# Three query groups of 128 and a 64-wide tail in one PV pass per pair, and a cubic exponential on VectorE for four tiles per batch entry

## The chip, the cores and the metric

The kernel runs on one core of a Trainium2 chip. The metric is the device time of one execution in microseconds. Each execution also records the mean clock that TensorE was granted, as a share of full speed.

A ratio below is the mean time of one kernel's fast runs over the mean of the fast runs of the kernel before from the same rounds on the same chip, so it isn't quite the ratio of the medians quoted beside it. Runs over 1.5% above the fastest run of the same kernel are called slow. On one core no second die tells whether such a run was disturbed from outside.

## The reference, cut to what matters

```python
def _attn_ref(q, k, v, cap):            # 8 batch entries, 12 heads, 448 rows, 64 wide
    scores = scale * np.matmul(q, k.transpose(0, 1, 3, 2))
    scores = cap * np.tanh(scores / cap)          # cap = 30
    attn = np.exp(scores - max);  attn /= attn.sum(-1)
    return np.matmul(attn, v)

def _moe_ref(x, phi, w1, w2):           # x: 3584 x 768, the attention output
    logits = x @ phi                              # 32 slots
    d = softmax of logits over the rows; slot_input = d.T @ x
    ...                                           # small two-layer MLP per expert, softmax over slots
```

Most of the time is attention: one tanh and one exponential for each of 8 x 12 x 448 x 448 elements, on ScalarE.

## The kernel before

Heads are worked in pairs, keys in tiles of 64. Two heads' 64 keys fill 128 partitions, so `ex` holds, for one key tile of a pair, 128 partitions by 448 queries. Six tiles make a step, 42 tiles (seven steps) make one batch entry, here called a period. The program order in the source is the order on each engine: there is no scheduler that moves instructions. VectorE's trace shows that order: the copy to kT started at 121.45 us, behind the polynomial operation that stands ahead of it, though its transposes had been issued from 120.09 to 120.61.

One step, on ScalarE two tanh and an exponential, on TensorE two passes of the PV product and two batches of score matmuls, with slots "a" to "d" for everything else:

```python
for j in range(NCH):
    tanh_chunk(2 * j); tanh_chunk(2 * j + 1); exp_chunk(j - 1)   # ScalarE
    pv_pass(pr, 0)                       # 14 matmuls, then rec and xq on VectorE
    run(j, "a")                          # x_transp; first part of the polynomial
    qk_chunk(2 * j + 2)                  # 6 score matmuls
    run(j, "b")
    pv_pass(pr, 1)                       # 14 matmuls, then rec and xq on VectorE
    run(j, "c")                          # second part of the polynomial
    qk_chunk(2 * j + 3)
    run(j, "d")                          # slot sums, zacc, transposes of K, fillers
```

The 448 queries are cut into four groups of 128 which overlap (offsets 0, 128, 256, 320); a mask keeps the doubled queries out of the softmax over rows. `spare(n)` issues n junk matmuls on TensorE ("fillers"). VectorE takes the exponential of one tile off ScalarE in some steps:

```python
shared = [j ... if j % 7 in (1, 3) and j > 7]

def poly_exp(j, part):                   # part 0: three operations (split into exponent and mantissa)
    ...
    elif part == 1:                      # two operations
        dve.scalar_tensor_tensor(xp, xm, POW2[1], xm, ALU.add, ALU.mult)
        dve.scalar_tensor_tensor(xp, xp, POW2[2], xm, ALU.add, ALU.mult)
    else:                                # two operations, a step later
        ...
for j in shared:
    for slot, part in (("a", 0), ("c", 1)):
        at(j, slot, poly_exp, j, part)
```

The small products (transposes of Q, K and x, logits, slot sums `slps`, row sums `zps`) all take their PSUM tile from a pool with a single buffer, psT; VectorE empties it each time. PV has a single bank too, psV.

The softmax here doesn't subtract the row's maximum and nothing guards it: scores larger than these inputs give would overflow.

## Time and profile before

| what | before |
|---|---|
| median time, 5 runs | 315.88 us (315.54 to 315.99) |
| mean granted clock | 0.981 |
| ScalarE / TensorE / VectorE busy | 89% / 87% / 61% |
| one period (42 key tiles) | 32.29 us, ScalarE without a gap |

The first two lines are the busy time of each engine on the page of the kernel before and the granted clock in 40 slices of the span, in tenths. It is at full until the very end.

```profile
PE 272.0 (87%) x4071; PEld 190.5 (61%) x4071; DVE 191.0 (61%) x478; ACT 278.9 (89%) x209; POOL 137.5 (44%) x178
PEclk9999999999999999999999999999999999999975
```

And a table by stage: one line for each step of a period, cut where the first score matmul of the step starts. After the colon-separated window come its length, the busy time of each engine with its number of instructions, the granted clock, the DMA share and GB/s. Shown are steps 5 and 6, and the sum over all seven steps.

```profile
core 0: us, PE busy (x) PEld busy (x) DVE busy (x) ACT busy (x) POOL busy (x), PEclk, DMA share, GB/s
126.61:131.72 5.11, 4.56 (x71) 3.31 (x71) 2.44 (x8) 5.11 (x4) 2.42 (x4) 1.00 1.06 204
131.72:136.14 4.42, 4.17 (x64) 3.01 (x62) 2.32 (x8) 4.42 (x4) 2.65 (x4) 1.00 1.17 175
...
sum 32.29, PE 29.39 PEld 21.03 DVE 21.78 ACT 32.29 POOL 16.96; mean PE 4.20 PEld 3.00 DVE 3.11 ACT 4.61 POOL 2.42
```

ScalarE is busy for the whole window, 32.29 of 32.29 us. TensorE is busy for 29.39 of them, at full clock.

### The profile page before, as it was taken

Reading aid. Unit: us, or ns where it says so; the run is one execution under the profiler, and the core shown is the slowest. Engines: PE = TensorE matmul, PEld = TensorE weight load, DVE = VectorE, ACT = ScalarE, POOL = GpSimd, SP = SyncE. Lnnn points to the kernel's source line nnn. Section 1 sums busy time; section 2 is a strip of 40 time slices with the busy share of each in tenths; the row PEclk is TensorE's granted clock in tenths of the full one; section 3 lists DMA queues with packets and bytes.
Section 4 is the critical chain, followed back from the end, with each engine's and each line's share of the span. In section 5 each row is a group of like instructions: output and inputs, shape, how many; then the busy total and the mean of one; then the engine's idle time right before and its main releaser. Section 6 shows DMA issues by size and latency. Waiting matters only on the chain.

```text
span 313.8 us, 9354 instructions
## 1 busy us (share of the span) xinstructions
PE 272.0 (87%) x4071; PEld 190.5 (61%) x4071; DVE 191.0 (61%) x478; ACT 278.9 (89%) x209; POOL 137.5 (44%) x178
## 2 busy tenths in 40 slices
PE   8899998989899989898989998989898898998710
PEld 6676666666676666666666666666676578643300
DVE  3624567846785578457855885578657765335830
ACT  4999999999999999999999999999999999226720
POOL 5593662655455654474457426652753020000000
PEclk9999999999999999999999999999999999999975
DMA  7999999799999999999999999999899829959996
GB/s 257 209 205 194 205 200 231 121 184 230 228 154 199 232 212 147 194 184 207 160 182 224 205 178 189 220 217 180 147 208 190 208 62 309 357 207 332 393 413 244
DMA packets 57481, 67.64 MB, mean 216 GB/s; under 512 B 3808, under 2 KB 53600, under 8 KB 57440
## 3 DMA queue, kind: packets, MB, share of 16 engines
q0 software_dynamic: 42448, 35.31, 73.5%
q1 hardware_dynamic: 14704, 31.50, 29.0%
q8 instruction: 32, 0.52, 0.6%
q10 hardware_dynamic: 288, 0.23, 0.2%
q14 instruction: 9, 0.07, 0.1%
HBM read 91.32 MB, written 18.87 MB: 351 GB/s over the span
## 4 chain that ended last, share of the span: by engine, by line
ACT 69%; PE 19%; DVE 5%; DMA 2%; issue 2%; DVEq 0%; ACTq 0%
ACT ex L291 36%; ACT ex L295 32%; PE pv L331 4%; DMA out_dram<-ob 2%; PE sc L282 2%; PE so_ps L690 2%; PE hp L662 2%; PE junk L521 2%; PE op L726 1%; PE boot L521 1%; DVE xq L342 1%; PE op L770 1%; ACT ob L779 1%; PE xps L357 1%; PE pvm L331 1%
## 5 line engine op out<-in xcount | busy, mean ns | idle before, releaser
L291 ACT ACTIVATE ex<-sc 128x1344 bf16<-128x1344 f32 (+1 forms) x113 | 163.7, 1719 | 0.8 <-PE sc L282 0.8
L295 ACT ACTIVATE ex<-ex 128x2688 bf16<-128x2688 bf16 (+4 forms) x58 | 158.0, 2753 | 0.1
L331 PEld LDWEIGHTS <-ex 128*128 128x128 bf16 x1344 | 78.0, 97 | 23.7 <-DVE xq L342 13.7
L331 PE MATMUL pv<-vbd,ex 128*128 128x130 bf16 x1274 | 89.2, 220 | 2.6 <-DVE xq L342 0.8
L282 PE MATMUL sc<-qT,kT 64*64 64x448 bf16 x672 | 78.6, 358 | 5.0 <-ACT ex L291 4.3
L260 POOL CAST vbd<-vraw 64x896 bf16<-64x896 f32 x23 | 22.4, 974 | 64.9 <-PE pv L331 49.8
L385 POOL COPY e<-E 128x512 bf16<-128x512 bf16 x9 | 6.7, 746 | 83.3 <-ACT E L379 49.2
L341 DVE RECIPROCAL rec<-pv 128x4 f32<-128x4 f32 x91 | 16.5, 182 | 42.6 <-PE pv L331 42.6
L342 DVE TENSOR_TENSOR xq<-pv,rec 128x256 bf16<-128x256 f32 x91 | 38.6, 424 | 3.1
L282 PEld LDWEIGHTS <-kT 64*64 64x64 bf16 x672 | 26.9, 105 | 22.2 <-issue 4.2
L521 PEld LDWEIGHTS <-ones 128*128 128x128 bf16 x428 | 26.0, 101 | 10.6 <-DVE xq L342 6.0
L521 PE MATMUL junk<-ones 128*128 128x128 bf16 x391 | 29.1, 220 | 3.1 <-DVE xq L342 2.6
L252 DVE COPY kT<-kps 128x896 bf16<-128x896 bf16 x23 | 14.3, 623 | 18.2 <-PE kps L250 18.0
L261 POOL CAST vbd<-vraw 64x896 bf16<-64x896 f32 x23 | 23.9, 1041 | 1.3
L109 POOL DMA_DIRECT2D w1b<-in_moe_w_dram x32 | 24.5, 766 | 0.0
L359 DVE COPY xT<-xps 128x512 bf16<-128x512 bf16 x47 | 19.5, 414 | 1.0 <-PE xps L357 1.0
L357 PE MATMUL xps<-ident,xq 128*128 128x128 bf16 x188 | 18.1, 218 | 0.8 <-DVE zacc L396 0.2
L172 POOL DMA_DIRECT2D qb<-in_q_dram x22 | 16.2, 737 | 3.9 <-DMA kraw<-in_k_dram 3.2
L252 DVE COPY qT<-qps 128x896 bf16<-128x896 bf16 x23 | 14.2, 618 | 5.5 <-PE qps L250 5.5
L250 PE MATMUL qps<-ident,qb 128*64 128x128 bf16 x308 | 12.8, 222 | 4.1 <-DVE lg L373 4.0
L172 POOL DMA_DIRECT2D kb<-in_k_dram x22 | 16.0, 727 | 0.0
L113 POOL DMA_DIRECT2D w2d<-in_moe_w_dram x20 | 15.1, 761 | 0.0
(117 smaller groups left out, 280.7 us busy)
## 6 DMA issues: line engine op xcount, KB each, us to landing
w1b<-in_moe_w_dram POOLq DMA_DIRECT2D x32, 384.0 KB, 8.5
vraw<-in_v_dram SPq DMA_DIRECT2D x23, 448.0 KB, 6.0
w2d<-in_moe_w_dram POOLq DMA_DIRECT2D x20, 384.0 KB, 9.4
w2t<-w2d SPq DMA_DIRECT2D x20, 384.0 KB, 5.2
out_dram<-ob SPq DMA_DIRECT2D x8, 768.0 KB, 8.5
qb<-in_q_dram POOLq DMA_DIRECT2D x22, 224.0 KB, 7.4
kb<-in_k_dram POOLq DMA_DIRECT2D x22, 224.0 KB, 7.8
w2b<-in_moe_w_dram POOLq DMA_DIRECT2D x12, 384.0 KB, 8.9
```

The costliest lines, as they stand in the source:

```text
L109: pool.dma_start(out=w1b[e][:, js, fs], in_=w1r[:, e, js, fs])
L172: (sp if nm == "v" else pool).dma_start(out=t, in_=quad_ap(nm, Q))
L252: dve.tensor_copy(t, ps)
L260: pool.tensor_copy(t[0:HP, :, :, 0:DH], raw[0:HP])
L261: pool.tensor_copy(t[HP:P, :, :, DH + 1:VW - 1], raw[HP:P])
L282: pe.matmul(sc[cs, u, 0:S], qkT["k", Q][r, c, cs], qkT["q", Q][r, :, cs], start=True, stop=True)
L291: act.activation(exs[j][:, half * CS + u0:half * CS + u1, :], sc[:, u0:u1, 0:S], ACT.Tanh, scale=qk_scale / cap)
L295: act.activation(exs[j][:, u0:u1, :], exs[j][:, u0:u1, :], ACT.Exp, scale=cap)
L331: pe.matmul(pvs[pr, half][:, n, 0:VW], exs[j][:, u, GOFF[g]:GOFF[g] + P], vbds[Q % 2][:, h, c, :], start=(c == 0 and n == 0), stop=(c == N ...
L342: dve.tensor_tensor(xq[Q][:, 2 * half:2 * half + 2, h * P:(h + 1) * P] .rearrange("p g (i d) -> p g i d", i=2), pv[:, :, :, 0:DH], rec.to_ ...
L357: pe.transpose(ps[:, g, :], xq[Q][:, g, h * P:(h + 1) * P], ident)
L521: pe.matmul(junk if home is None else home, ones, ones, start=True, stop=True)
```

## The change

Its intent: drop the overlap of the query groups (three groups of 128 plus a tail of 64 whose two heads sit on the two halves of the partitions), so that one PV pass per pair and one normalising pass are enough; make the polynomial one degree lower; and use the VectorE time won to take four tiles per period off ScalarE instead of two.

```diff
-GOFF = (0, 128, 256, 320)
+NF = 3;  TAIL = NF * P
-POW2 = (0.013534163, -0.157022653, 12.3105704, 23.0539684, 37.6797712)
+POW2 = (0.0780246108, -0.102619004, 6.12336670, 5.79476321)
-shared = [... if j % 7 in (1, 3) and j > 7]
+shared = [... if j % 7 in (1, 3, 4, 6) and j > 7]
         else:
-            dve.scalar_tensor_tensor(xp, xp, POW2[3], xm, ALU.add, ALU.mult)
-            dve.scalar_tensor_tensor(t, xp, POW2[4], xe.bitcast(F32), ALU.add, ALU.mult)
+            dve.scalar_tensor_tensor(t, xp, POW2[3], xe.bitcast(F32), ALU.add, ALU.mult)
...
+    def pv_rest(pr):
+        pv_mms(pr, CA, NT, (0, 1, 2), pvs[pr])            # 3 tiles x 3 groups of 128x130
+        for c0, c1 in ((0, CA), (CA, NT)):
+            pv_mms(pr, c0, c1, (NF,), pvs[pr][:, 2 * NF:NT, :])   # 14 tails of 64x65
+        norm(pr, 0, NT, pvs.pop(pr))                      # one pass over 448 columns
...
-            pv_pass(pr, 0)
+            pv_first(pr)                                  # 4 tiles x 3 groups
...
-            pv_pass(pr, 1, ...)
+            pv_rest(pr)
```

The transposes of x, the logits, the row sums and the slot sums follow the new grouping, and the mask goes (cut).

More of the change, by code (lines that the diff above doesn't have):

```diff
@@ L24 @@
 NG = 4
-GOFF = (0, 128, 256, 320)
-VW = 2 * (DH + 1)
-MASKED = -30000.0
-POW2 = (0.013534163, -0.157022653, 12.3105704, 23.0539684, 37.6797712)
+NF = 3
+TAIL = NF * P
+W = DH + 1
+VW = 2 * W
+POW2 = (0.0780246108, -0.102619004, 6.12336670, 5.79476321)
 @with_exitstack
@@ L78 @@
     pool.memset(ones32[0:NS, :], 1.0)
-    mask = consts.tile([P, NG, NS], F32, name="mask")
-    pool.memset(mask, 0.0)
-    pool.memset(mask[0:HP, NG - 1, :], MASKED)
     phib = consts.tile([P, NJ, NS], BF16, name="phib")
@@ L298, in exp_chunk @@
         exp_part(j, 1 if j in shared else 0, CH)
-    shared = [j for j in range(NCH - 2) if j % 7 in (1, 3) and j > 7] if cap < 80 else []
+    shared = [j for j in range(NCH - 2) if j % 7 in (1, 3, 4, 6) and j > 7] if cap < 80 else []
     def poly_exp(j, part):
@@ L315, in poly_exp, with pv_mms @@
         else:
-            dve.scalar_tensor_tensor(xp, xp, POW2[3], xm, ALU.add, ALU.mult)
-            dve.scalar_tensor_tensor(t, xp, POW2[4], xe.bitcast(F32), ALU.add, ALU.mult)
-    def pv_tiles(pr, half, c0, c1, home=None):
+            dve.scalar_tensor_tensor(t, xp, POW2[3], xe.bitcast(F32), ALU.add, ALU.mult)
+    def pv_mms(pr, c0, c1, gs, dst):
         Q, h = divmod(pr, 2)
-        if c0 == 0:
-            if h == 0 and half == 0:
-                xq[Q] = xs.tile([P, NG, 2 * P], BF16, name="xq", tag="xq")
-            pvs[pr, half] = psV.tile([P, 2, VW], F32, name="pv", tag="pv") \
-                if home is None else home
-        for c in range(c0, c1):
-            j, u = divmod(pr * NT + c, CH)
-            for n in range(2):
-                g = 2 * half + n
-                pe.matmul(pvs[pr, half][:, n, 0:VW],
-                          exs[j][:, u, GOFF[g]:GOFF[g] + P],
-                          vbds[Q % 2][:, h, c, :],
-                          start=(c == 0 and n == 0), stop=(c == NT - 1),
-                          skip_group_check=True)
@@ L337, in norm @@
-    def norm(pr, half):
-        Q, h = divmod(pr, 2)
-        pv = pvs.pop((pr, half))[:, :, 0:VW].rearrange("p g (i w) -> p g i w", i=2)
-        rec = xs.tile([P, 2, 2, 1], F32, name="rec", tag="rec", bufs=4)
-        dve.reciprocal(rec, pv[:, :, :, DH:DH + 1])
-        dve.tensor_tensor(
-            xq[Q][:, 2 * half:2 * half + 2, h * P:(h + 1) * P]
-            .rearrange("p g (i d) -> p g i d", i=2),
-            pv[:, :, :, 0:DH],
-            rec.to_broadcast([P, 2, 2, DH]), op=ALU.mult)
@@ L348, in pv_pass @@
-    def pv_pass(pr, half, home=None):
-        pv_tiles(pr, half, 0, NT, home)
-        norm(pr, half)
-    def x_transp(pr):
-        Q, h = divmod(pr, 2)
-        ps = psT.tile([P, NG, P], BF16, name="xps", tag="T")
-        for g in range(NG):
-            pe.transpose(ps[:, g, :], xq[Q][:, g, h * P:(h + 1) * P], ident)
-        t = xs.tile([P, NG, P], BF16, name="xT", tag="xT", bufs=2)
+        for tail in (False, True):
+            for c in range(c0, c1):
+                j, u = divmod(pr * NT + c, CH)
+                for g in gs:
+                    if (g == NF) != tail:
+                        continue
+                    for n in range(2 if tail else 1):
+                        r = slice(n * HP, n * HP + HP) if tail else slice(0, P)
+                        q0, s0 = g * P, 2 * (g - gs[0])
+                        out_, v_ = (dst[r, s0, :], vbds[Q % 2][r, h, c, n * W:n * W + W]) \
+                            if tail else (dst[:, s0:s0 + 2, :], vbds[Q % 2][:, h, c, :])
+                        pe.matmul(out_, exs[j][r, u, q0:q0 + (HP if tail else P)], v_,
+                                  start=(c == 0 and g == gs[0]), stop=(c == NT - 1),
+                                  skip_group_check=True)
@@ new lines, in norm, with xq_tile @@
+    def norm(pr, s0, s1, pv):
+        Q, h = divmod(pr, 2)
+        rec = xs.tile([P, NT, 1], F32, name="rec", tag="rec", bufs=4)[:, 0:s1 - s0, :]
+        dve.reciprocal(rec, pv[:, 0:s1 - s0, DH:W])
+        dve.tensor_tensor(xq[Q][:, h, s0:s1, :], pv[:, 0:s1 - s0, 0:DH],
+                          rec.to_broadcast([P, s1 - s0, DH]), op=ALU.mult)
+    def xq_tile(pr):
+        Q, h = divmod(pr, 2)
+        if h == 0:
+            xq[Q] = xs.tile([P, 2, NT, DH], BF16, name="xq", tag="xq")
+    CA = 4
@@ new lines, in pv_first, with turn_x @@
+    def pv_first(pr):
+        xq_tile(pr)
+        pvs[pr] = psV.tile([P, NT, W], F32, name="pv", tag="pv")
+        pv_mms(pr, 0, CA, (0, 1, 2), pvs[pr])
+    def pv_rest(pr):
[3 more added lines that the diff above has]
+        norm(pr, 0, NT, pvs.pop(pr))
+    def turn_x(ps, q0, pr, gs):
+        Q, h = divmod(pr, 2)
+        for g in gs:
+            c0 = g * P - q0
+            if g < NF:
+                pe.transpose(ps[:, c0:c0 + P],
+                             xq[Q][:, h, 2 * g:2 * g + 2, :].rearrange("p i d -> p (i d)"), ident)
+                continue
+            for n in range(2):
+                r = slice(n * HP, n * HP + HP)
+                pe.transpose(ps[r, c0:c0 + HP], xq[Q][r, h, NT - 1, :], ident[r, r])
@@ L359, in x_transp, with phi_mms @@
+    def x_transp(pr):
+        ps = psT.tile([P, S], BF16, name="xps", tag="T")
+        turn_x(ps, 0, pr, range(NG))
+        t = xs.tile([P, S], BF16, name="xT", tag="xT", bufs=2)
         dve.tensor_copy(t, ps)
         xTs[pr] = t
+    def phi_mms(dst, t, g, jt, first, last):
+        if g < NF:
+            pe.matmul(dst, t[:, g * P:(g + 1) * P], phib[:, jt, :], start=first, stop=last,
+                      skip_group_check=True)
+            return
+        for n in range(2):
+            pe.matmul(dst[n * HP:n * HP + HP], t[:, TAIL:S], phib[:, jt, :], start=first,
+                      stop=last, skip_group_check=True)
@@ L367, in logits @@
             for h in range(2):
-                pe.matmul(ps[:, g, :], xTs[2 * Q + h][:, g, :],
-                          phib[:, 2 * hq + h, :], start=(h == 0), stop=(h == 1))
+                phi_mms(ps[:, g, :], xTs[2 * Q + h], g, 2 * hq + h, h == 0, h == 1)
         xTs.pop(2 * Q), xTs.pop(2 * Q + 1)
@@ L372, in logits @@
             lgs[b] = xs.tile([P, NG, NS], F32, name="lg", tag="lg", bufs=2)
-        dve.tensor_tensor(lgs[b], ps, mask if hq == 0 else lgs[b], op=ALU.add)
+            dve.tensor_copy(lgs[b], ps)
+        else:
+            dve.tensor_tensor(lgs[b], ps, lgs[b], op=ALU.add)
     es, e4s = {}, {}
@@ L391, in e_norm @@
         for g in range(NG):
-            pe.matmul(ps, e4s[b][:, g, :], ones[:, 0:1], start=(g == 0), stop=(g == NG - 1))
+            r = slice(0, P if g < NF else HP)
+            pe.matmul(ps, e4s[b][r, g, :], ones[r, 0:1], start=(g == 0), stop=(g == NG - 1))
         if b == 0:
@@ L402, in e_transp @@
         ps = psT.tile([P, 512], BF16, name="eps", tag="T")
-        for g in (3, 0, 1, 2):
-            pe.transpose(ps[:, GOFF[g]:GOFF[g] + P], e4s[b][:, g, :], ident)
+        for g in range(NG):
+            n = P if g < NF else HP
+            pe.transpose(ps[:, g * P:g * P + n], e4s[b][0:n, g, :], ident[0:n, 0:n])
         dve.tensor_copy((ETl if b >= B - 2 else ET4[:, b // 2])[:, :, b % 2, :],
@@ L415, in e_sums, with slot_mms @@
         dve.reciprocal(winv[:, bb, :], ps)
-    def slot_mms(b, ps, gs, jts=None):
+    def slot_mms(b, ps, gs):
         for g in gs:
             for jt in range(NJ):
-                pe.matmul(ps[:, jt, :],
-                          xq[b * NQB + jt // 2][:, g, (jt % 2) * P:(jt % 2 + 1) * P],
-                          es[b][:, g, :], start=(g == 0 and jt == 0), stop=(g == NG - 1),
-                          skip_group_check=True)
+                x = xq[b * NQB + jt // 2][:, jt % 2, :, :]
+                if g < NF:
+                    pe.matmul(ps[:, jt, :], x[:, 2 * g:2 * g + 2, :].rearrange("p i d -> p (i d)"),
+                              es[b][:, g, :], start=(g == 0 and jt == 0), stop=False,
+                              skip_group_check=True)
+                    continue
+                for n in range(2):
+                    r = slice(n * HP, n * HP + HP)
+                    pe.matmul(ps[r, jt, :], x[r, NT - 1, :], es[b][r, g, :],
+                              start=False, stop=True, skip_group_check=True)
     def slot_sums(b):
@@ L446, in spare @@
     def spare(n):
-        busy(n, psV.tile([P, 2, VW], F32, name="junk", tag="pv")[:, 0, 0:P])
+        busy(n, psV.tile([P, P], F32, name="junk", tag="pv"))
     PER = 2 * NQB * NT // CH
@@ L549 @@
         if pr is not None:
-            pv_pass(pr, 0)
+            pv_first(pr)
         run(j, "a")
         if j == NCH - 1:
-            pv_pass(pr, 1)
+            pv_rest(pr)
             busy(8, psT.tile([P, P], F32, name="filler", tag="T"))
@@ L563 @@
         if pr is not None:
-            pv_pass(pr, 1, psT.tile([P, 2, VW], F32, name="pvt", tag="T")
-                    if pr == 0 else None)
+            pv_rest(pr)
         run(j, "c")
@@ L580, in bank @@
         return big.tile(shape, dt, name=name, tag="b")
-    pvm = [bank([P, 2, VW], name=f"pvm{half}") for half in range(2)]
-    pv2 = [bank([P, 2, VW], name=f"pvl{half}") for half in range(2)]
+    halves = [(0, 1), (2, NF)]
+    cuts = (0, 4, NT)
+    pvm = [bank([P, 4, W], name=f"pvm{half}") for half in range(2)]
+    pv2 = [bank([P, 4, W], name=f"pvl{half}") for half in range(2)]
     junk = bank([P, P], name="junk")
-    pv_tiles(last - 1, 0, 0, NT, pvm[0])
-    norm(last - 1, 0)
-    logits(NQ - 2)
-    pv_tiles(last - 1, 1, 0, NT, pvm[1])
-    norm(last - 1, 1)
-    for half in range(2):
-        pv_tiles(last, half, 0, NT - CH + CL, pv2[half])
-    x_transp(last - 1)
-    for half in range(2):
-        pv_tiles(last, half, NT - CH + CL, NT - 1)
-    for half in range(2):
-        pv_tiles(last, half, NT - 1, NT)
-        norm(last, half)
+    xq_tile(last - 1)
+    for half, gs in enumerate(halves):
+        pv_mms(last - 1, 0, NT, gs, pvm[half])
+        norm(last - 1, cuts[half], cuts[half + 1], pvm[half])
+        if half == 0:
+            logits(NQ - 2)
+    for half, gs in enumerate(halves):
+        pv_mms(last, 0, NT - CH + CL, gs, pv2[half])
+    x_transp(last - 1)
+    for half, gs in enumerate(halves):
+        pv_mms(last, NT - CH + CL, NT - 1, gs, pv2[half])
+    for half, gs in enumerate(halves):
+        pv_mms(last, NT - 1, NT, gs, pv2[half])
+        norm(last, cuts[half], cuts[half + 1], pv2[half])
     busy(5)
-    xl = xs.tile([P, NG, P], BF16, name="xT", tag="xT", bufs=2)
-    halves = [range(0, 2), range(2, 4)]
+    xl = xs.tile([P, S], BF16, name="xT", tag="xT", bufs=2)
     Q, bl = NQ - 1, B - 1
@@ L612 @@
         for g in gs:
-            pe.matmul(lps[s][:, g - 2 * s, :], xTs[2 * Q][:, g, :], phib[:, NJ - 2, :],
-                      start=False, stop=False, skip_group_check=True)
+            phi_mms(lps[s][:, g - 2 * s, :], xTs[2 * Q], g, NJ - 2, False, False)
     for s, gs in enumerate(halves):
-        hs = slice(2 * s, 2 * s + 2)
-        ps = bank([P, 2, P], BF16, name="xpl")
-        for g in gs:
-            pe.transpose(ps[:, g - 2 * s, :], xq[Q][:, g, P:2 * P], ident)
-        act.copy(xl[:, hs, :], ps)
+        q0, q1 = 2 * s * P, min(2 * s * P + 2 * P, S)
+        ps = bank([P, 2 * P], BF16, name="xpl")
+        turn_x(ps, q0, last, gs)
+        act.copy(xl[:, q0:q1], ps[:, 0:q1 - q0])
         busy(3)
     for s, gs in enumerate(halves):
-        hs = slice(2 * s, 2 * s + 2)
         for g in gs:
-            pe.matmul(lps[s][:, g - 2 * s, :], xl[:, g, :], phib[:, NJ - 1, :],
-                      start=False, stop=True, skip_group_check=True)
-        act.activation(el[:, hs, :], lps[s], ACT.Exp)
+            phi_mms(lps[s][:, g - 2 * s, :], xl, g, NJ - 1, False, True)
+        act.activation(el[:, 2 * s:2 * s + 2, :], lps[s], ACT.Exp)
     for gs in halves:
```

## The prediction

> **What bounds the kernel now.** I read the page first (busy shares, chain of waits), then the timeline of each engine over one period. A period is one batch entry b: 42 key tiles, worked off as seven steps of six tiles. I number the steps 0 to 6 by j mod 7. In each step ScalarE does two tanh of three tiles and one exponential of six (five where VectorE takes one over). TensorE does one PV pass, the score matmuls for the first half of a later step, another PV pass, and those for the second half.
>
> ```profile
> ACT 69%; PE 19%; DVE 5%; DMA 2%; issue 2%; DVEq 0%; ACTq 0%
> ```
> The chain is ScalarE's until about 222 us and then TensorE's. The period from 100.14 to 132.43 us on ScalarE, steps 3 to 5:
>
> ```profile
> 115.67 2.85 ACT L291 ACTIVATE ex<-sc 128x1344 bf16<-128x1344 f32 x2
> 118.02 2.85 ACT L295 ACTIVATE ex<-ex 128x2688 bf16<-128x2688 bf16 x1
> 120.35 0.71 ACT L379 ACTIVATE E<-lg 128x128 bf16<-128x128 f32 x1
> 120.55 2.87 ACT L291 ACTIVATE ex<-sc 128x1344 bf16<-128x1344 f32 x2
> 122.89 2.49 ACT L295 ACTIVATE ex<-ex 128x2240 bf16<-128x2240 bf16 x1
> 124.85 2.89 ACT L291 ACTIVATE ex<-sc 128x1344 bf16<-128x1344 f32 x2
> ```
> The starts, not the durations, give the rate, because the instructions overlap: two tanh 2.35, full exponential 2.33, short one 1.96 us. There is no gap, so ScalarE sets the 32.29 us period. But TensorE has little to spare: it waits for a score buffer (on ScalarE) only 0.3 to 1.0 us a period. Step 6 turning into step 0, on TensorE and then VectorE:
>
> ```profile
> 101.02 0.76 PE L282 MATMUL sc<-qT,kT 64*64 64x448 bf16 x6
> 101.70 0.25 PE L392 MATMUL zps<-ones,e 128*128 128x1 bf16 x4
> 102.21 0.58 PE L250 MATMUL kps<-ident,kb 128*64 128x128 bf16 x14 [0.25 <-DVE zacc L396]
> 102.72 0.98 PE L331 MATMUL pv<-vbd,ex 128*128 128x130 bf16 x14
> 103.53 0.39 PE L357 MATMUL xps<-ident,xq 128*128 128x128 bf16 x4
> 103.85 0.57 PE L282 MATMUL sc<-qT,kT 64*64 64x448 bf16 x6
> ```
> ```profile
> 101.12 0.18 DVE L341 RECIPROCAL rec<-pv 128x4 f32<-128x4 f32 x1 [0.84 <-PE pv L331]
> 101.34 0.42 DVE L342 TENSOR_TENSOR xq<-pv,rec 128x256 bf16<-128x256 f32 x1
> 101.99 0.16 DVE L396 TENSOR_TENSOR zacc<-zps,zacc 128x1 f32<-128x1 f32 x1 [0.23 <-PE zps L392]
> 102.83 0.62 DVE L252 COPY kT<-kps 128x896 bf16<-128x896 bf16 x1 [0.67 <-PE kps L250]
> ```
> TensorE and VectorE pass one PSUM bank (zps, kps, xps, lps, eps, slps, all in a pool of one buffer) back and forth: kps starts 0.06 us after zacc ends. VectorE runs in program order, so anything long put before such a copy stops TensorE. An example with the polynomial, step 1 (contended) and step 3 (not):
>
> ```profile
> 111.08 0.80 DVE L313 SCALAR_TENSOR_TENSOR xp<-xm 128x448 f32<-128x448 f32 x1
> 111.91 1.25 DVE L314 SCALAR_TENSOR_TENSOR xp<-xp,xm 128x448 f32<-128x448 f32 x1
> 120.26 0.62 DVE L313 SCALAR_TENSOR_TENSOR xp<-xm 128x448 f32<-128x448 f32 x1
> 120.91 0.62 DVE L314 SCALAR_TENSOR_TENSOR xp<-xp,xm 128x448 f32<-128x448 f32 x1
> 121.45 0.62 DVE L252 COPY kT<-kps 128x896 bf16<-128x896 bf16 x1
> ```
> ```profile
> 110.29 1.11 POOL L260 CAST vbd<-vraw 64x896 bf16<-64x896 f32 x1 [3.32 <-PE pv L331]
> 111.46 1.24 POOL L261 CAST vbd<-vraw 64x896 bf16<-64x896 f32 x1
> ```
> The pair of polynomial operations takes 2.01 us beside a GpSimd cast of V, 1.19 us alone.
>
> [...]the kT copy at 121.45 waited for L314 though kps had been issued from 120.09 to 120.61. [...]14 PV matmuls take 0.81 us to the next start before xps (same mode) and 0.91 before the scores (64*64). [...]24 slot matmuls at 124.53 take 0.61 us, 25 ns each.
>
> **The change, part by part.** (1) ScalarE. Shared tiles go from 14 to 27 (steps 1, 3, 4, 6 instead of 1, 3). Each shortens an exponential by 2.33 - 1.96 = 0.37 us: 13 x 0.37 = 4.8 us over the run; a period with four falls to 32.29 - 0.74 = 31.55 us.
>
> (2) PV on TensorE. A pair loses 7 full matmuls (58 ns each, 0.41 us) and gains 14 of 64x65. The K transposes in the small mode go at 0.51/14 = 36 ns; on separate row groups I take 30 ns: 14 x 30 = 0.42. Even. The tails stand next to the scores, which are 64*64 too[...]. The first part (12 matmuls) takes 0.70 us, the rest 9 x 58 + 100 + 420 = 1.04 us.
>
> (3) Small TensorE parts: 60 more matmuls a period in all, 42 of them the tails. Logits +0.2, slots +0.3 us (more matmuls, mode changes).
>
> (4) Normalising: two passes (0.56 us of VectorE each, start to next) become one over 448 columns. [...]one pass costs 0.76 us. Six pairs save 6 x 0.36 = 2.2 us a period, and the wait in the middle of a pair disappears.
>
> (5) Polynomial: first part, three operations, 1.16 us (109.37 to 110.53); second part 1.19 or about 2.0; last part now one operation, 0.62. Two more tiles add about 2 x 3.3 us and two dropped operations save 1.3. VectorE goes from 22.0 to about 25 us of a 31.5 us period: not full, but what matters is the order.
>
> In the built program the order of the changed kernel on VectorE in step 6 is xT, three polynomial operations, rec, xq, two polynomial operations, zacc, kT. In step 4: xT, last part, three operations, rec, xq, two operations, slacc. GpSimd's casts of V fall into steps 1, 4 and 6, right behind PV, so the second part is contended in both new steps.
>
> Now from the first score matmul of one step to that of the next (before, from the trace; after, worked by hand with the hand-over of 0.06 us to TensorE and 0.1 us back):
> - step 3 to 4: before 4.56, after 4.68 (longer multiply ahead of the kT copy).
> - 4 to 5: before 4.17. After: xT, last part and first part fill VectorE until 2.13; norm to 2.9; contended second part to about 4.4; slacc 4.75; xps, scores: 5.1.
> - 5 to 6: before 5.11. After: PV rest ends 1.63, q transposes 2.15, norm frees VectorE at 2.5, qT done 3.1, eps and ET to 4.0, logits, PV first, xps: 5.4.
> - 6 to 0: before 4.42. After: norm to 2.5, second part to 4.2 to 4.5, zacc, then kps 4.3 to 5.2, kT, xps: 5.9 to 6.3.
> - 0 to 1: before 4.75, after 4.9. 1 to 2: 4.48, after 4.4. 2 to 3: 4.80, after 4.4 (one operation fewer ahead of lg).
>
> Sum before: 32.29, ScalarE's pace. After: about 34.9 against ScalarE's 31.55. So the TensorE-VectorE loop would be the bound, 2.6 us a period slower than now. A score buffer may come late by 0.7 (after q transposes) to about 1.5 us before ScalarE stops, which shifts the first loss but not the rate. Six full periods (j from 8 on; the first has no polynomial) give 15.6 us, the last step 4 at the end about 1: 315.9 + 16.6 = 332.
>
> **The rivals.** (A) ScalarE stays the bound and the lag is absorbed: 315.9 - 4.8 = 311. For it: gapless ScalarE now, and VectorE only 80% busy. Against it: in step 6 alone kps moves from 1.2 to about 2.8 us after PV ends, where the slack is 0.7. (B) The loop lengthens, but tails cost less than 30 ns and casts miss the second part (1.2 us): my steps then sum to about 33.3, 315.9 + 6 x 1.0 = 322. (C) Tails cost 60 ns, as if nothing overlapped: 0.42 more a pair, 2.5 a period where TensorE is the pace: towards 340. The 36 ns of the small-mode transposes speak against it. (D) The chain after 267 us changes: only a few norms and small matmuls, under 1 us.
>
> **Range and chances.** The hand chain gives 332, its mild form 322, ScalarE's bound 311. I lean on the chain but not on all of it, since each step has 0.2 us of guess and the rival forms lie below: 326 us, 8 in 10 between 314 and 334. The 2% line is at 309.6 and 322.2. Faster needs more than the whole 4.8 us on ScalarE: 0.04. Within 2%: 0.30. Slower: 0.66.
>
> **What would show it.** Right: the chain of waits moves from ScalarE to TensorE and VectorE; ScalarE shows idle time at tanh, released by the score matmuls, mostly in steps 0, 1 and 6; kps waits on zacc for 1.5 us or more; periods of 33 to 35 us. The group of the second polynomial part shows a mean near 0.8 and 1.1 us. Wrong: ScalarE without gaps and a period near 31.6; PV tails far from 30 ns; or kps not behind the second part.

## The result, and the profile after

| | before | after |
|---|---|---|
| median of 5 runs | 315.88 us | 359.16 us (356.37 to 367.9) |
| ratio of fast runs | | 1.134 (1.130 to 1.138) |
| mean granted clock | 0.981 | 0.91 in the fast runs, 0.87 in the profiled one |

The changed kernel is correct and 13% slower; the prediction's range ended at 334. The profiled run was the slowest of the five (366.1 us from first to last instruction). What I read from it below is a pattern, not a size; sizes are taken from runs with a steady clock.

These are lines of the page of the changed kernel: ScalarE's busy tenths, the granted clock, the engines of the chain that ended last, and the group of the tanh.

```profile
ACT  4999999659967699549967699548988998623740
PEclk9999999559975799559976899558999999999995
PE 54%; DVE 28%; ACT 13%; issue 2%; DVEq 0%; ACTq 0%
L289 ACT ACTIVATE ex<-sc 128x1344 bf16<-128x1344 f32 (+1 forms) x113 | 141.5, 1298 | 50.7 <-PE pv L330 42.4
```

The second line was flat before. Now it dips to half several times, and each dip of ScalarE's line sits under or next to one. The chain moved from ScalarE (69% before) to TensorE and VectorE, as predicted. ScalarE stood still for 50.7 us ahead of its tanh (0.8 us before). The tanh writes into one of four `ex` buffers, and PV is what frees them: the page puts 42.4 us down to PV and only 7.2 to the score matmuls, which the prediction had named as the releaser. The same table by stage for steps 5 and 6, with the sum of the period:

```profile
146.35:154.48 8.13, 7.65 (x84) 5.11 (x83) 3.06 (x7) 4.99 (x4) 1.19 (x2) 0.52 1.13 203
154.48:162.98 8.50, 7.02 (x73) 4.85 (x73) 4.80 (x10) 4.91 (x4) 5.39 (x7) 0.50 0.25 62
...
sum 41.04, PE 35.51 PEld 24.18 DVE 25.48 ACT 32.22 POOL 17.73; mean PE 5.07 PEld 3.45 DVE 3.64 ACT 4.60 POOL 2.53
```

The two steps run at a clock of 0.52 and 0.50, and take 8.13 and 8.50 us instead of 5.11 and 4.42. TensorE is nearly always busy in step 5 (7.65 of 8.13 us): this isn't waiting, its work takes longer. What went ahead of the fall is on TensorE's timeline (the bracket is the idle time before the group and what ended it):

```profile
144.72 0.84 PE L330 MATMUL pv<-vbd,ex 128*128 128x130 bf16 x12 [1.11 <-POOL vbd L259]
146.09 0.33 PE L365 MATMUL xps<-ident,xq 128*128 128x128 bf16 x3 [0.52 <-DVE slacc L467]
...
160.35 0.96 PE L248 MATMUL kps<-ident,kb 128*64 128x128 bf16 x14 [1.48 <-DVE zacc L425]
```

In step 4 TensorE waits twice within 2.5 us. The profile puts the first wait down to GpSimd's cast of V, because that ended last (144.61); the norm, which frees the single PV bank, ended at 144.57. It is the norm that counts: in a variant below without a tile in step 4, the same PV group started at 130.63, 0.2 us after the norm (130.41) and well before the cast ended (131.49). What made the norm late, and slacc and zacc after it, is on VectorE's timeline:

```profile
142.79 1.00 DVE L309 TENSOR_SCALAR xe<-xe 128x448 int32<-128x448 int32 x1
...
145.14 0.62 DVE L312 SCALAR_TENSOR_TENSOR xp<-xp,xm 128x448 f32<-128x448 f32 x1
145.68 0.35 DVE L467 TENSOR_TENSOR slacc<-slps,slacc 128x192 f32<-128x192 f32 x1
...
158.97 1.25 DVE L312 SCALAR_TENSOR_TENSOR xp<-xp,xm 128x448 f32<-128x448 f32 x1
160.15 0.15 DVE L425 TENSOR_TENSOR zacc<-zps,zacc 128x1 f32<-128x1 f32 x1
```

VectorE does exactly what the prediction said it would: the second part of the polynomial stands ahead of slacc in step 4 and ahead of zacc in step 6, and TensorE's next product into psT starts when slacc or zacc frees the bank: xps at 146.09 us where slacc ended at 146.03, kps at 160.35 where zacc ended at 160.30. Cut into stretches of 3.5 us, the same place one period later reads:

```profile
184.00:187.50 3.50, 1.87 (x46) 1.54 (x44) 3.00 (x6) 3.50 (x3) 3.44 (x5) 1.00 1.20 182
187.50:191.00 3.50, 3.50 (x47) 2.31 (x44) 1.69 (x4) 1.31 (x2) 1.03 (x2) 0.52 1.13 229
```

TensorE was busy for only 1.87 of 3.50 us, and in the next stretch the clock is at half. The clock reads 1.00 or 0.50 wherever a stretch lies wholly in one state, and the six stretches at half during attention, with their edges interpolated within the quarter of a microsecond in which the clock changes, last 17.07 (three times), 10.24, 3.41 and 20.48 us in this run. These are 5, 5, 5, 3, 1 and 6 times one length of 3.413 us (an estimate from them: 20.48 / 6), which I call a clock window below.

So there were two theories for the missing time. Theory 1: the chain through VectorE is as predicted, and its waits also trip the clock, which the prediction never considered. Theory 2: the new grouping of PV (more and smaller matmuls, mode changes) is slow by itself, and the clock with it. Against both stands a third: that the clock comes from outside, from a bad chip or moment.

### The profile page after: what moved, and what is told of

It reads as the page before. It is cut to its first block, busy times and chain, and to the rows that moved or that the text cites.

```text
span 366.1 us, 10324 instructions
## 1 busy us (share of the span) xinstructions
PE 306.5 (84%) x4551; PEld 207.6 (57%) x4551; DVE 211.4 (58%) x450; ACT 279.7 (76%) x209; POOL 138.9 (38%) x176
## 4 chain that ended last, share of the span: by engine, by line
PE 54%; DVE 28%; ACT 13%; issue 2%; DVEq 0%; ACTq 0%
PE pv L330 16%; PE sc L280 10%; ACT ex L289 6%; DVE xq L338 5%; ACT ex L293 5%; PE junk L557 5%; DVE xp L312 4%; DVE xp L311 3%; PE xps L365 3%; DVE xe L309 3%; PE qps L248 3%; PE kps L248 2%; PE xps L370 2%; PE so_ps L723 2%; PE lps L382 2%
## 5 line engine op out<-in xcount | busy, mean ns | idle before, releaser
L289 ACT ACTIVATE ex<-sc 128x1344 bf16<-128x1344 f32 (+1 forms) x113 | 141.5, 1298 | 50.7 <-PE pv L330 42.4
L293 ACT ACTIVATE ex<-ex 128x2688 bf16<-128x2688 bf16 (+4 forms) x58 | 128.1, 2212 | 0.1
L330 PE MATMUL pv<-vbd,ex 128*128 128x130 bf16 (+1 forms) x1610 | 100.3, 228 | 9.2 <-POOL vbd L259 7.8
L330 PEld LDWEIGHTS <-ex 128*128 128x128 bf16 (+1 forms) x1680 | 84.3, 111 | 40.7 <-issue 33.4
L280 PE MATMUL sc<-qT,kT 64*64 64x448 bf16 x672 | 93.4, 398 | 1.3 <-ACT ex L289 1.1
L376 DVE COPY xT<-xps 128x448 bf16<-128x448 bf16 x47 | 18.3, 390 | 38.1 <-PE xps L370 38.1
L338 DVE TENSOR_TENSOR xq<-pv,rec 128x448 bf16<-128x448 f32 x46 | 28.7, 625 | 1.6
L312 DVE SCALAR_TENSOR_TENSOR xp<-xp,xm 128x448 f32<-128x448 f32 x27 | 25.1, 929 | 0.9
L248 PE MATMUL kps<-ident,kb 128*64 128x128 bf16 x308 | 14.7, 242 | 10.0 <-DVE zacc L425 8.6
L311 DVE SCALAR_TENSOR_TENSOR xp<-xm 128x448 f32<-128x448 f32 x27 | 17.5, 648 | 0.0
```

Of the source, the lines that this page charges most:

```text
L248: pe.transpose(ps[h * HP:h * HP + HP, c, :], src[:, h, c * DH:(c + 1) * DH], ident)
L280: pe.matmul(sc[cs, u, 0:S], qkT["k", Q][r, c, cs], qkT["q", Q][r, :, cs], start=True, stop=True)
L289: act.activation(exs[j][:, half * CS + u0:half * CS + u1, :], sc[:, u0:u1, 0:S], ACT.Tanh, scale=qk_scale / cap)
L293: act.activation(exs[j][:, u0:u1, :], exs[j][:, u0:u1, :], ACT.Exp, scale=cap)
L330: pe.matmul(out_, exs[j][r, u, q0:q0 + (HP if tail else P)], v_, start=(c == 0 and g == gs[0]), stop=(c == NT - 1), skip_group_check=True)
L338: dve.tensor_tensor(xq[Q][:, h, s0:s1, :], pv[:, 0:s1 - s0, 0:DH], rec.to_broadcast([P, s1 - s0, DH]), op=ALU.mult)
```

## The experiments

Sixteen kernels ran, all with correct results, three rounds each (four runs of each kernel with the profiled one). The kernel before ran beside them each time at 315.6 to 315.8 us, which already speaks against the third theory. Edits are against the changed kernel unless the text says otherwise.

### Which part of the change costs the time?

**Two tiles again, everything else kept.**

```diff
-    shared = [... if j % 7 in (1, 3, 4, 6) and j > 7]
+    shared = [... if j % 7 in (1, 3) and j > 7]
```

> The changed kernel with the regrouping and the cubic kept, but only the old two tiles per period on VectorE (steps 1 and 3). Theory 1 (the two extra tiles, placed in steps 4 and 6 ahead of the small copies that TensorE waits for, make the loop long and let TensorE idle so that its clock is granted at half): without them the clock stays at 1.00 through the attention and the time is that of before, 315 to 317 us. Theory 2 (the regrouping, with its 480 more matmuls and its mode changes, is what costs): the time stays well above 330 us.

Measured: 317.69 us, ratio 1.009 (1.005 to 1.013), clock 0.98, no dip. The grouping, the single norm and the cubic cost 1.8 us together (2.0 against the kernel before of the same rounds, 315.65 us), and don't touch the clock. Theory 2 falls. Part of the 1.8 us is in the tail of attention, where ScalarE waits longer for the last transposes of x; this is ScalarE's line of waits (total, times, longest) of the kernel before, then of this one:

```profile
ACT xT L620 <- PE xpl L619: 1.8, 1, 1.8
```
```profile
ACT xT L655 <- PE xpl L365: 3.4, 1, 3.4
```

**The kernel before with the cubic and four tiles.** Old groups, two PV passes:

```diff
-    (1, 3)            # in before
+    (1, 3, 4, 6)      # and the new POW2, with the merged last operation
```

> The kernel before, with its 4 x 128 groups and two passes, given the cubic and four tiles per period. Theory 1: the same wait of the K transposes on the zacc copy and the same half clock appear, 345 us or more, since the two-pass kernel has no less work on VectorE. Theory 2: the tiles are harmless, so the time is at or under 316 us.

Measured: 352.03 us, ratio 1.099 from the two fast runs (345.42 and 347.95 us; the other two took 356), clock 0.91 to 0.95 from run to run. So the four tiles with the cubic, without any of the new grouping, bring most of the loss: the wait of the K transposes on zacc reached 2.2 us, and in its profiled run the clock fell five times before the end of attention.

### Is it the clock, and what lowers it?

**The waits filled with junk matmuls.** VectorE's order is untouched; TensorE gets 49 fillers a period, in the places where it waits.

```diff
+        if 0 < b < B - 1:
+            at(j + 6, "d", spare, 22)         # before the K transposes
+            at(j + 11, "d", fill, 18)         # before the slot sums
             at(j + 11, "d", slot_sums, b)
+            at(j + 11, "d", spare, 9)         # after them
```

> The changed kernel with 49 meaningless matmuls added per period, in the places where TensorE sat idle in steps 4 and 6 (18 ahead of the slot sums, 9 ahead of the next PV, 22 ahead of the K transposes). Nothing waits for them. Theory 1: TensorE no longer idles there, the granted clock stays at 1.00, and what is left is the loop at full clock, the 34.9 us a period of the hand chain or a little more: 328 to 338 us, although there is more work. Theory 3 (the loop is as long as it is because of waits, and the half clock only fills time that would be waited anyway): no better than 355 us.

(The recorded text's theory 3 is not the third theory above, but that the half clock costs nothing of its own.) Measured: 341.77 us, ratio 1.085, clock 0.98 to 0.99. The granted clock of its page:

```profile
PEclk9999999999999999999999999999999999999975
```

More work on TensorE made the kernel 17.4 us faster (359.16 to 341.77), because it held the clock (0.98 to 0.99 against 0.91). It came out above the 328 to 338 us that I expected, since the loop itself is longer than my hand chain had it (by step, further below). The junk itself costs little: from step 4 to 5, which both kernels run at full clock, the loop takes 5.80 us with it and 5.69 without. This run splits the loss: about 1.8 us for the grouping (two tiles), about 24.1 us for the chain through VectorE at full clock (341.77 - 317.69), about 17.4 us for the clock; what the junk costs is counted with the chain.

**The kernel before with nothing but a delay.** The kernels so far differed in grouping and polynomial. These take the unchanged kernel before and put 2, 4 or 6 fills of a scratch tile on VectorE ahead of zacc in step 6 of six periods (measured at 432 ns each), the last also with junk matmuls in the wait:

```diff
+        for _ in range(2):                    # or 4, or 6; in e_norm, in before
+            dve.memset(xp, 0.0)
         if b == 0:
             dve.tensor_copy(zacc, ps)
```
```diff
+        if 0 < b < B - 1:                     # fourth run only, with 6 fills
+            at(j + 6, "d", spare, 26)
```

> The kernel before with two VectorE fills of a scratch tile (an estimated 0.43 us each) ahead of zacc in step 6 of six periods. The K transposes should wait about 0.9 us instead of 0.25. If a single wait must come to about 1.5 us in 3.5 us to lower the clock: clock stays at 0.98, 316 to 318 us. If any wait near 1 us lowers it: half-clock stretches and over 320.

> The same with four fills: a wait of about 1.75 us. If idleness summed over a stretch of some 3.5 us decides, and where the stretch begins is chance: the clock falls in some periods and not in others, different from run to run, mean clock 0.94 to 0.98, 320 to 332 us. If waits cannot lower the clock without the changed grouping or polynomial: clock 0.98, 319 to 323.

> The same with six fills: a wait of about 2.6 us. If idleness decides: the clock falls in most of the six periods, mean clock 0.90 to 0.95, 330 to 345 us. If not: clock 0.98, 323 to 328.

> Six fills as in the run before, and 26 junk matmuls on TensorE in five of the waits. If idleness lowers the clock: clock at 0.97 or above, 322 to 329 us, although VectorE is as late as before. If the delay itself (VectorE's load) lowers it: the same time and clock as without the junk matmuls.

| fills | longest wait on zacc | time | clock of the four runs |
|---|---|---|---|
| 0 (before) | 0.3 us | 315.62 us | 0.98 |
| 2 | 1.0 us | 317.07 us | 0.979 to 0.983 |
| 4 | 2.1 us | 332.53 us | 0.945 to 0.965 |
| 6 | 3.3 us | 342.46 us | 0.934 to 0.941 |
| 6, with junk matmuls | 1.8 us | 331.30 us | 0.972 to 0.982 |

Windows of 3.5 us around the wait, in the kernels with 2, 4 and 6 fills:

```profile
99.50:103.00 3.50, 2.55 (x34) 1.58 (x36) 2.24 (x7) 3.50 (x3) 1.80 (x2) 1.00 1.18 184
```
```profile
103.00:106.50 3.50, 1.36 (x23) 0.83 (x21) 2.35 (x7) 3.50 (x4) 3.03 (x4) 1.00 1.24 203
106.50:110.00 3.50, 3.50 (x38) 2.48 (x34) 1.56 (x4) 2.22 (x1) 1.79 (x3) 0.51 1.20 266
```
```profile
142.50:146.00 3.50, 0.64 (x10) 0.30 (x7) 2.63 (x7) 3.50 (x4) 3.46 (x5) 0.96 0.99 158
```

With TensorE busy for 2.55 of 3.50 us the clock stays; with 1.36 the next stretch runs at 0.51. With four fills the clock fell after the wait in all six periods of the profiled run, and came back after 3.5 us five times and after 7 us once. Six waits of one microsecond cost 1.5 us in all, six of two microseconds 16.9: six more microseconds of waiting cannot be that step. The last run closes it: with VectorE just as late but junk matmuls in the wait (in all six waits, not five), the clock is back and 11.2 us are won, though 331.30 us is above the 322 to 329 that I expected. The wait left there is 1.8 us, and its profiled run still shows one fall in six: that wait lies near the edge. That idleness of TensorE lowers the clock, in the kernel before as in the changed one, is thereby shown.

### Which of the waits trips it?

**Three variants with one of the two new steps disarmed.** First the tile of step 4 left out (tiles 1, 3, 6), then the tile of step 6 (tiles 1, 3, 4), then all four tiles with only step 4's second part moved behind slacc:

```diff
-    (1, 3, 4, 6)
+    (1, 3, 6)                                 # first;  (1, 3, 4) second
```
```diff
-        for slot, part in (("a", 0), ("c", 1)):
+        for slot, part in (("a", 0), ("d" if j % 7 == 4 else "c", 1)):     # third
```

> The changed kernel with tiles in steps 1, 3 and 6 only, in their old places. The wait of the K transposes on zacc in step 6 stays, about 1.5 us. At full clock the hand chain gives about 34.0 us a period, 325 to 330 us. If one wait of 1.5 us in a period is enough to halve the clock, some periods are longer and it lies between 330 and 345 us.

> The changed kernel with tiles in steps 1, 3 and 4 only, in their old places. What is left are the two waits of step 4 (1.1 us ahead of PV, 0.5 us ahead of the x transposes); in the full change the clock fell right after these. At full clock the hand chain gives about 33.9 us a period, 324 to 330 us. If these two waits are what makes the clock fall, it falls here too, once a period, but comes back within about 4 us since step 6 has no long wait: 328 to 340 us.

> The changed kernel with only step 4's second part moved behind slacc; step 6 stays as in the change. If the pair of waits in step 4 (1.1 us on the norm and 0.5 us on slacc) is what trips the clock, removing the second of them keeps it at full: about 326 to 331 us, with the wait of the K transposes on zacc of 1.5 us or more still there, clock 0.97 or above. If the wait of step 6 trips it by itself: half-clock stretches stay, 340 us or more.

| variant | waits left in a period | time (runs) | clock |
|---|---|---|---|
| no step 4 | 2.1 on zacc | 331.16 (329.01 to 335.37) | 0.965 to 0.980 |
| no step 6 | 1.1 and 0.5 in step 4 | 357.14 (335.13 to 361.27) | 0.863 to 0.971 |
| step 4's second part late | 1.1 in step 4, 2.1 on zacc | 346.03 (343.34 to 348.88) | 0.929 to 0.957 |

Three of the four runs of the second variant count as slow by the rule above, so it has no ratio; its clock differs from run to run, and even its fastest run stands at 335.13 us. I had expected one culprit, the pair of waits in step 4, for the third kernel 326 to 331 us, and for the second a fall of about 4 us a period and at most 340 us. Both expectations failed: both places can do it. In the profiled run of the first variant the clock fell in one period of six, though the wait was about the same in all. This stretch of it has TensorE busy for 1.60 us and was not followed by a fall:

```profile
105.50:109.00 3.50, 1.60 (x33) 1.36 (x35) 2.43 (x4) 3.43 (x3) 3.42 (x5) 1.00 1.23 205
```

But I cut this stretch by hand, and the clock windows lie elsewhere. The clock record shows where: in each trace with falls, all changes of the clock lie whole multiples of 3.413 us apart (in the changed kernel 5, 12, 17, 24, 29, 36, 39, 40, 41, 48 and 54 windows after the fall at 64.78 us). In this variant one boundary is at 106.15 us. The gap from 105.35 to 107.40 us was shared by two windows, with TensorE busy for 2.60 and 2.16 of 3.41 us, and the clock held. The gap from 70.01 to 72.07 us lay all but 0.06 us in one window, with 1.41 us busy, and the clock fell at 72.01. The other four gaps straddle a boundary too, and none had a fall. In this trace, then, the gap that lay in one window was followed by a fall, and the five that were shared by two were not.

The runs also differ in length of the fall: after step 4's waits the clock mostly stayed low for 10.2 to 20.5 us, after the one wait on zacc for 3.4 to 6.8. Busy time doesn't tell these apart: two windows of the changed kernel at half clock were both busy for 3.41 of 3.41 us, and the clock stayed low after the first (187.66 to 191.07 us) and came back after the second (194.49 to 197.90). At full clock, the windows just ahead of this run's falls were busy for 1.36 to 2.04 us, but the clock also held after one with 1.85 (279.82 to 283.23). What goes along with it is the work done. For each matmul that starts in a window, take the columns it streams times the share of the 128x128 array that it uses; add up, with the shapes and windows of all 18 profiled traces (1309 windows, from 18 us on to about the end of attention). All 56 windows under 2590 were followed by half the clock and all 1135 over 3240 by full, whichever clock they ran at themselves; the 118 between went both ways. The two windows above count 2742 and 2908. At half clock a window holds less work: in the changed kernel, from 20 to 290 us, a median of 2616 (998 to 3558) against 4189 at full. This is a pattern in the traces; no run varied the work of a window at the same busy time. That a kernel near this edge can stay low because of it is my reading, and was not shown.

### Is the rest VectorE's order?

**All four tiles, the second part behind slacc and zacc.**

```diff
-        for slot, part in (("a", 0), ("c", 1)):
+        for slot, part in (("a", 0), ("d" if j % 7 in (4, 6) else "c", 1)):
```

> The changed kernel with the second polynomial part of steps 4 and 6 moved from before to behind the small copies (slacc; zacc and kT) in VectorE's order. Same work, no extra matmul. Theory 1: the K transposes no longer wait on zacc for more than 0.5 us, the clock stays at 1.00 or nearly, and by the same hand chain a period takes about 33 us: 315 to 325 us. If VectorE's total load is the cause and not its order: unchanged, over 350 us.

Measured: 324.38 us, ratio 1.028 (1.026 to 1.030), clock 0.98 to 0.99: 34.8 us of the loss gone with the same instructions in another order. TensorE at the K transposes, then VectorE:

```profile
71.42 0.58 PE L248 MATMUL kps<-ident,kb 128*64 128x128 bf16 x14 [0.25 <-DVE zacc L423]
```
```profile
71.21 0.16 DVE L423 COPY zacc<-zps 128x1 f32<-128x1 f32 x1
72.04 0.62 DVE L250 COPY kT<-kps 128x896 bf16<-128x896 bf16 x1 [0.67 <-PE kps L248]
```

The wait on zacc is back at the 0.25 us of the kernel before. The 1.1 us wait in step 4 stayed, and the clock held: one such wait a period did not lower it here. Moving step 3's second part as well:

> The changed kernel with all four tiles, second part late in steps 3, 4 and 6, all fillers. If VectorE's order is what costs, a little better than the run with only steps 4 and 6 late: 319 to 324 us. If the remaining wait is VectorE's sheer amount of work in step 4 (the first part ahead of the norm), the same as that run: 323.5 to 325.

It gave 320.76 us (ratio 1.016; one of its four runs took 326.94), within the expected 319 to 324. Four tiles thus stay slower than before in every order I tried; the first part of step 4 still stands ahead of the norm.

### Is there a version that beats both?

**Fewer fillers.** With the second part late in all new steps, I took out 30 of the 36 fillers a period, to give TensorE room, once with four tiles and once with three:

```diff
-        at(j + 1, "d", spare, 10);  at(j + 2, "a", spare, 14);  at(j + 2, "c", spare, 8);  at(j + 3, "d", spare, 4)
+        at(j + 2, "a", spare, 6)
```

> Four tiles; the second polynomial part of steps 3, 4 and 6 behind the small copies; 30 of the 36 filler matmuls a period taken out. The fillers now stand in a loop that sets the pace, so taking them out should shorten steps 1 to 3 by 1.0 to 1.5 us and the late part of step 3 another 0.5: a period between ScalarE's 31.55 and 32.2 us, 311 to 317 us, if the clock stays at 1.00. If the fillers are needed to keep the clock, it falls in steps 1 to 3 and the time is over 330 us.

> As the kernel with four late tiles, but three (steps 1, 3, 6), so without the contended first part of step 4. ScalarE's period is 31.92 us and no step should exceed it by much: 313 to 315.5 us with a full clock; over 330 if the clock falls in steps 1 to 3.

Neither reached its time: 347.35 us (clock 0.84 to 0.90, two of four runs slow), where the other branch of the expectation, over 330 us, came true; and 319.26 us (0.92 to 0.94, one run slow), where neither branch did. The fillers look like waste, and they are what keeps the clock up in steps 2 and 3: in a period of the three-tile run it was at half from 115.28 to 125.5 us, between the starts of step 2 (113.80) and step 4 (126.09), and with all fillers kept, in the next run, it is at 0.98.

**Three tiles (1, 3, 6), second part late, all fillers kept,** in the changed kernel and in the kernel before with the cubic:

> The changed kernel with three shared tiles (steps 1, 3, 6), the second part of the polynomial behind slacc or zacc in steps 3 and 6, and all fillers of the kernel before kept. If the half clock of the run with fewer fillers was due to the missing fillers: clock at 0.98 or above, ScalarE nearly gapless at 31.9 us a period, 315 to 317.5 us (before, minus 2 us for the third tile in six periods, plus the 2 us that the regrouping costs at start and end). If three tiles themselves lower the clock: over 318 with half-clock stretches.

> The kernel before (4x128 groups, two passes) with the cubic and three shared tiles (1, 3, 6), second part late in steps 3 and 6, all fillers. If ScalarE is the bound and the late order keeps VectorE off the path: 313.5 to 316 us, at full clock. If VectorE's norms between the passes leave no room: 317 to 325.

Measured: 315.57 us, ratio 1.002 (0.998 to 1.006), and 315.01 us, ratio 0.9975 (0.996 to 0.999), both at a clock of 0.98 (one run of the first took 318.1, at a clock of 0.986). The second is ahead of the kernel before by a hair, 0.25%, which the 2% line counts as the same. With the new grouping, the loss of the two-tile run (2.0 us) and the gain of the third tile cancel.

## Why the prediction was wrong

By its own steps:

- **The bound and where it would move.** Right. The chain went from ScalarE to TensorE and VectorE, the second part of the polynomial stood ahead of slacc and zacc, and the K transposes waited 1.5 to 2.1 us on zacc ("1.5 us or more"). The late order, the one edit that undoes just this, gave back 34.8 us.
- **PV tails, the norm.** Right, the tails a bit dear: the 23 matmuls of the second pass took 0.95 us where 1.04 was expected, so a tail is near 24 ns (an estimate, with the prediction's 58 ns a full matmul and 100 ns for mode changes, 0.91 less 0.81 us in the trace of the kernel before), not 30, which was a guess of mine below the 36 ns of the K transposes. The multiply of the norm took 625 ns over 448 columns, against 424 over 256 before, and the whole pass 0.77 us in step 4 (143.72 to 144.49 us); the 0.76 was my estimate.
- **The sum by steps.** This is the step that failed, and with it "Range and chances". It took every TensorE duration from the kernel before, so it assumed the clock of the kernel before, and listed four rivals of which none had another clock. It counted a wait of TensorE as its own length and nothing more; measured, the clock that these waits lowered costs 17.4 us. The same sum was also about 10 us short at full clock (341.77 against 332). From the first score matmul of one step to that of the next:

| step | before | predicted | after (profiled) | waits filled, full clock |
|---|---|---|---|---|
| 4 to 5 | 4.17 | 5.1 | 5.69 | 5.80 |
| 5 to 6 | 5.11 | 5.4 | 8.13 | 5.54 |
| 6 to 0 | 4.42 | 5.9 to 6.3 | 8.50 | 6.18 |
| 0 to 1 | 4.55 | 4.9 | 4.77 | 4.40 |
| 1 to 2 | 4.69 | 4.4 | 4.49 | 4.49 |
| 2 to 3 | 4.80 | 4.4 | 4.61 | 4.62 |
| 3 to 4 | 4.55 | 4.68 | 4.85 | 4.84 |
| period | 32.29 | 34.9 | 41.04 | 35.87 |

  (Before is one period of its trace, so its rows 0 to 1 and 1 to 2 differ by 0.2 us from the text on record, which took another.) At full clock the hand chain was off by 1 us in 35; the other 5.2 us of the period are the half clock, 4.9 of them in steps 5 and 6.
- **Step 4 to 5, a term mis-sized even at full clock.** I let GpSimd's cast collide with the second part of the polynomial, which has two inputs in SBUF. In step 4 it collided one operation earlier: the third operation of the first part, with one input, took 1.00 us at 142.79 against a median of 0.395, beside the cast at 142.46. From the step's start at 140.66 the norm ended after 3.9 us instead of 2.9, and the second part after 5.1 instead of 4.4. The collision is 0.6 us of that; the rest is a slip of the sum, since the third operation only starts at 2.13 us, where the hand chain has it end. Since the cast missed the second part in step 4, the means that the prediction gave for its two operations, near 0.8 and 1.1 us, came out at 0.65 and 0.93. I had counted on a collision only for the operations that the trace of the kernel before had shown longer beside a cast (0.80 and 1.25 us against 0.62).
- **The chain at the end**, "under 1 us": 1.8 us with two tiles.
- **The range.** I had 332 by the chain and drew it down to 326 towards milder forms. With the clock held it takes 341.77. The pull was in the wrong direction: here the hand chain had left waits out, not invented any.

## What to carry to other kernels

TensorE, made to wait, also became slower here: before counting a new wait of TensorE as its own length, ask how much work TensorE will get over the next few microseconds, because idle stretches of 1.6 to 2.1 us in 3.5 often halved the clock, for 3.4 to 20.5 us (TensorE busy for 1.87 of 3.50 us in the changed kernel and for 1.36 with four fills; after 1.60 in the variant without step 4 it held). Junk matmuls in a tuned kernel may be holding that clock (without 30 of the 36 a period it fell to 0.84 to 0.90 with four tiles), so take them out only with the granted clock in view. And where a single buffer couples two engines, the order of instructions on the one that frees it can be worth nearly as much as their number: the same instructions in another order gave 324 us instead of 359, two tiles fewer gave 318.
